# A small group's first matrix in matmuls of 512 columns, and one of its weight splits handed to a DMA

## The chip, the cores and the metric

The kernel runs on one core of a Trainium2 chip. The time is that of one execution on the device, in microseconds (us), and a kernel's time is the median of several executions. Columns of a matmul are the elements of the moving operand for each of the 128 partitions; the stationary operand is the weight that is loaded into the array ahead of it.

## The reference

```
x   = attention(q, packed keys)                       # [2304, 512]
x   = silu(x @ w_in) @ w_out                          # [2304, 512]
P   = sinkhorn(exp(x @ w_gate))                       # [2304, 8], eight rounds
out = 0
for e in range(8):
    h    = maximum(x @ w1[e], 0)                      # 512 -> 1024
    out += P[:, e:e+1] * (h @ w2[e])                  # 1024 -> 512
```

All of it is in float32. The kernel holds a float32 operand as a high part (`h`, in the matrix engine's type float32r) and a low part (`l`, what the high part leaves), and makes a product of three: high by high, high by low and low by high. An instruction of VectorE, `lo = raw - hi`, behind one of ScalarE, `hi = raw`, is called a split here (lines 144 and 145).

## The kernel before

The 2304 tokens of the last part are worked on in three groups: a small one of 256 tokens (two blocks of 128, called T0), and then two of 1024. The change is in the small group alone. It has 16 steps (`s` = 0 to 15, `G0` = 16): a step is one expert `e` and one half `fh` of its 1024 hidden columns, so each step has two weight matrices of 512 x 512, `w1` and `w2`, each loaded in two halves `j` of 256 rows (`load_w1`, `load_w2`, lines 773 to 787).

A step runs in four slots. Even slots run `up0(s, j)`, 24 matmuls of 256 columns (line 999): for two blocks `i` of 128 hidden rows and four blocks `k` of the 512 inputs, `wh` by `xs[0]` (the tokens' high part), `wh` by `xs[1]` (their low part) and `wl` by `xs[0]`. Behind them ScalarE makes the high part of the hidden values, `relu(ps)` (line 1002), and VectorE the low part, `max(ps, 0) - hi` (line 1003). Odd slots run `down0(s - 1, tt)` for one token block `tt`, 12 matmuls of 512 columns (line 1018), with the hidden values of the step before as stationary operand; the first six use what came of `up0(s - 1, 0)`, the last six what came of `up0(s - 1, 1)`. So TensorE is given up, down, up, down, and the hidden values of a step have some slots to be made in.

Each slot also takes one piece of other work. `w1_split(s + 1)` has its two halves in slots 0 and 1, `w2_split(s)` in slots 2 and 3 (of the last step, 15, in slots 0 and 1). In odd slots from step 1 on, `sinkhorn` takes one piece (about one round: a matmul `cs` with ones, line 1231, and eight small VectorE instructions). From step 9 on `x_forms` makes the sums of token blocks that the second group needs (lines 949 to 958, each followed by a split into `xf`); what is left of it is done at the end of step 14. The pieces of step 0 are made ahead, in `pre0`, beside the last matmuls of the stage before.

TensorE, VectorE and ScalarE run their instructions in exactly the order in which the code writes them (`manual_schedule`); the order of loads on the DMA queue of SyncE is the scheduler's. GpSimd has no work in this part. Buffers: 16 units of 128 x 1024 (`wp`) hold the split weights in turn, and `m` in PSUM holds two results of `up0` for each of the two `j`.

Of the kernel before, what the change touches and what calls it, by code (L numbers as in the profile page):

```python
# [14 lines left out]
ALU = mybir.AluOpType  # L15
# [89 lines left out]
def fused_kernel(  # L105
# [745 lines left out]
    def w1_split(s):  # L851
        w1t[s] = []
        for j in range(2):
            w1t[s].append(halves("w1", s, j, raw1[s, j]))
            if s + 1 < G0:
                load_w1(s + 1, j)
            yield
# [118 lines left out]
    xs, h0 = [], {}  # L976

    def pre0():

        t = [st["gh"].tile([128, 4, 256], F32R, tag="gh", name=f"xs{n}") for n in range(2)]  # L980
        xs.extend(t)
        for k in range(4):
            for n, (sb, c, _) in enumerate(T0):
                o = slice(128 * n, 128 * n + 128)
                split(t[0][:, k, o], t[1][:, k, o], x2[sb][k][:, c:c + 128])
            yield
        yield from w1_split(0)
        yield from w2_split(0)

    def up0(s, j):  # L990
        tag = "xz"[j]
        ps = st["m"].tile([128, 512], F32, tag=tag, name=f"u0{s}{j}").rearrange("p (i n) -> p i n", i=2)
        for i in range(2):
            n = 0
            f = slice(128 * (2 * j + i), 128 * (2 * j + i) + 128)
            for k in range(4):
                wh, wl = w1t[s][k // 2]
# [308 lines left out]
    with tc.manual_schedule(engines={mybir.EngineType.PE, mybir.EngineType.DVE, mybir.EngineType.Activation}):  # L1306
        for i, (c, b) in enumerate(seq):
# [14 lines left out]
            for half in range(2):  # L1322
# [3 lines left out]
                if c == NC - 1 and b == order[c][2] and half == 0:  # L1326
                    a2b_st.close()
                    open_("gh", 6)
# [66 lines left out]
    with tc.manual_schedule(engines={mybir.EngineType.PE, mybir.EngineType.DVE, mybir.EngineType.Activation}):  # L1395
# [12 lines left out]
        st["m"], s_ = pool("pm", 2, space=PSUM, side="left", reuse_waits="tile"); ctx.enter_context(s_)  # L1408
# [6 lines left out]
        for s in range(G0 + 1):  # L1415
            wb = w2_split(s) if 0 < s < G0 else iter(())
            wa = w1_split(s + 1) if s + 1 < G0 else wb
            for slot in range(4):
# [12 lines left out]
                next(wa if slot < 2 else wb, None)  # L1431
# [13 lines left out]
        for name in ("acc", "r2", "gh", "po"):  # L1445
            closers[name].close()
        for name, n in (("hb", 6), ("hi", 3), ("lo", 3), ("rb", 2)):
            open_(name, n, keep=True)
# [59 lines left out]
```

## Time and profile before

| | |
|---|---|
| median of 3 runs | 1784.09 us (1783.89 to 1784.69) |
| the profiled execution's own time | 1784.24 us |
| its span, from the first instruction to the last | 1782.5 us |
| TensorE busy | 1768.4 us, 99% of the span |
| VectorE busy | 1438.2 us, 81% |
| ScalarE busy | 1065.7 us, 60% |
| granted TensorE clock, as a share of full speed | 1.00 |

The times of the profiled execution and of the span differ by 1.7 us, which lie around the first and the last instruction. Matmuls overlap: one that is listed with 0.39 us may be followed by the next after 0.23 us, so the pace of TensorE is read from the starts of its matmuls and not from their durations.

### The profile page before, as it was taken

Reading aid. Unit: us, or ns where it says so; the run is one execution under the profiler, and the core shown is the slowest. Engines: PE = TensorE matmul, PEld = TensorE weight load, DVE = VectorE, ACT = ScalarE, POOL = GpSimd, SP = SyncE. Lnnn points to the kernel's source line nnn. Section 1 sums busy time; section 2 is a strip of 40 time slices with the busy share of each in tenths; the row PEclk is TensorE's granted clock in tenths of the full one; section 3 lists DMA queues with packets and bytes.
Section 4 is the critical chain, followed back from the end, with each engine's and each line's share of the span. In section 5 each row is a group of like instructions: output and inputs, shape, how many; then the busy total and the mean of one; then the engine's idle time right before and its main releaser. Section 6 shows DMA issues by size and latency. Waiting matters only on the chain.

```text
span 1782.5 us, 25390 instructions
## 1 busy us (share of the span) xinstructions
PE 1768.4 (99%) x9580; PEld 1509.7 (85%) x9580; DVE 1438.2 (81%) x1918; ACT 1065.7 (60%) x1694; POOL 1.0 (0%) x8
## 2 busy tenths in 40 slices
PE   8999999999999999999999999999999999999998
PEld 5899999989998888888888888888888888888887
DVE  7968796759676988899889999887777777777778
ACT  6766675644453666665666666656555555555555
POOL 0000000000000000000000000000000000000000
PEclk9999999999999999999999999999999999999999
DMA  9326676975664655465544455964454444545432
GB/s 363 129 95 214 247 262 249 331 255 172 221 210 161 229 180 183 160 203 186 199 162 171 172 186 196 322 222 167 155 174 165 154 154 147 170 155 172 148 130 95
DMA packets 141498, 341.75 MB, mean 192 GB/s; under 512 B 11952, under 2 KB 49472, under 8 KB 140480
## 3 DMA queue, kind: packets, MB, share of 16 engines
q1 hardware_dynamic: 141376, 340.14, 54.9%
q8 instruction: 75, 1.23, 0.3%
q14 instruction: 47, 0.39, 0.1%
HBM read 256.66 MB, written 83.44 MB: 191 GB/s over the span
## 4 chain that ended last, share of the span: by engine, by line
PE 95%; DVE 3%; ACT 1%; issue 1%; DMA 0%; DVEq 0%; SPq 0%; ACTq 0%
PE d L1106 34%; PE X L1154 20%; PE Z L1154 10%; PE g2w L689 8%; PE g L600 5%; PE Y L1154 5%; PE u L999 5%; PE d L1018 4%; PE g L654 3%; PE u L193 1%; PE s L193 0%; DMA kq<-in_kT_dram 0%; PE warm L203 0%; PE lg L1188 0%; DVE w2l L145 0%
## 5 line engine op out<-in xcount | busy, mean ns | idle before, releaser
L145 DVE TENSOR_TENSOR lo<-hb,hi 128x1024 fp32r<-128x1024 f32 x224 | 273.6, 1221 | 33.5 <-ACT hi L144 32.5
L1106 PE MATMUL d<-hi,w2f 128*128 128x512 f32 x896 | 294.2, 389 | 0.0
L1154 PE MATMUL X<-xf,w1l 128*128 128x512 f32 x1152 | 276.9, 389 | 0.0
L144 ACT CAST hi<-hb 128x1024 fp32r<-128x1024 f32 x224 | 235.3, 1052 | 64.8 <-PE d L1106 59.4
L1154 PEld LDWEIGHTS X<-xf,w1l 128*128 128x128 f32 x1152 | 216.2, 188 | 44.9
L1114 ACT COPY M<-d 128x512 f32<-128x512 f32 x234 | 137.3, 588 | 143.1 <-PE d L1106 139.8
L1118 DVE TENSOR_TENSOR M<-d,M 128x512 f32<-128x512 f32 x204 | 140.1, 687 | 100.6 <-PE d L1106 100.6
L1106 PEld LDWEIGHTS d<-hi,w2f 128*128 128x128 f32 x896 | 168.1, 188 | 34.9
L1106 PE MATMUL d<-lo,w2f 128*128 128x512 f32 x448 | 174.3, 389 | 0.0
L1106 PE MATMUL d<-hi,w2l 128*128 128x512 f32 x512 | 167.7, 389 | 0.0
L689 PE MATMUL g2w<-ring,woh 128*128 128x384 f32 x576 | 147.5, 337 | 0.0
L1102 ACT COPY d<-M 128x512 f32<-128x512 f32 x216 | 127.1, 590 | 20.9 <-DVE M L1118 19.5
L1106 PE MATMUL d<-hi,w2g 128*128 128x512 f32 x384 | 125.7, 389 | 0.0
L1106 PEld LDWEIGHTS d<-hi,w2l 128*128 128x128 f32 x512 | 96.2, 188 | 20.3 <-ACT d L1102 0.4
L689 PEld LDWEIGHTS g2w<-ring,woh 128*128 128x128 f32 x576 | 102.9, 188 | 8.6 <-issue 7.5
L1161 ACT COPY cp<-X 128x512 f32<-128x512 f32 x128 | 74.3, 581 | 46.5 <-PE X L1154 46.2
L1106 PE MATMUL d<-lo,w2l 128*128 128x512 f32 x256 | 99.6, 389 | 0.0
L1106 PEld LDWEIGHTS d<-lo,w2f 128*128 128x128 f32 x448 | 84.1, 188 | 17.5
L1154 PE MATMUL Y<-xf,w1f 128*128 128x512 f32 x384 | 97.3, 389 | 0.0
L689 PE MATMUL g2w<-ring,wol 128*128 128x384 f32 x288 | 96.3, 334 | 0.0
L999 PE MATMUL u<-xs,w1h 128*128 128x256 f32 x512 | 94.4, 285 | 0.0
L144 ACT CAST w1f<-rb 128x512 fp32r<-128x512 f32 x96 | 59.8, 624 | 54.9 <-PE d L1106 40.3
(220 smaller groups left out, 3482.0 us busy)
## 6 DMA issues: line engine op xcount, KB each, us to landing
r<-in_moe_w_dram SPq DMA_DIRECT2D x128, 512.0 KB, 3.9
w1l<-w1d SPq DMA_DIRECT2D x128, 512.0 KB, 4.2
w1d<-po SPq DMA_DIRECT2D x64, 512.0 KB, 4.4
w2d<-w2f SPq DMA_DIRECT2D x64, 512.0 KB, 4.1
w2l<-w2d SPq DMA_DIRECT2D x64, 512.0 KB, 3.6
rb<-in_moe_w_dram SPq DMA_DIRECT2D x96, 256.0 KB, 2.6
sb<-in_moe_w_dram SPq DMA_DIRECT2D x48, 256.0 KB, 2.7
pb<-pd SPq DMA_DIRECT2D x16, 512.0 KB, 5.2
```

The lines of the kernel that those rows point to most:

```text
L144: act.copy(out=hi, in_=raw)
L145: eng.tensor_tensor(out=lo, in0=raw, in1=hi.bitcast(F32), op=ALU.subtract)
L600: pe.matmul(ps, lhs[:, fs], rhs, start=(n == 0), stop=(n == 5))
L689: pe.matmul(ps[:, :TW], lhs[:, f % 2, ds], ring[f // 2][:, 2 * (f % 2) + rhs, q], start=(n == 0 and not on), stop=(n == 11), skip_group_ch ...
L999: pe.matmul(ps[:, i], w[:, k % 2, f], x[:, k], start=(n == 0), stop=(n == 11))
L1018: pe.matmul(ps, h[:, l, f % 2, 128 * tt:128 * tt + 128], w[:, f % 2], start=(fh == 0 and n == 0), stop=(fh == 1 and n == 11))
L1102: act.copy(out=ps, in_=m)
L1106: pe.matmul(ps, w[:, l, c, 128 * d:128 * d + 128], r[:, c], start=(n == 0 and not seed), stop=(n == 5), skip_group_check=seed)
L1114: act.copy(out=m, in_=ps)
L1118: dve.tensor_tensor(m, ps, m, op=ALU.add)
L1154: pe.matmul(ps, w[:, l, c, 128 * i:128 * i + 128], x[:, r, c], start=(n == 0 and p in (1, 7)), stop=(n == 5), skip_group_check=p in (2, 6, ...
L1161: act.copy(out=t, in_=ps)
```

## The change

`up0` multiplies each high weight by the tokens' high and low parts in one matmul of 512 columns: the two parts now lie side by side in one tile `xs`. The result has two halves of 256 columns; the low weight's matmul, still of 256 columns, is added into the first. A new `sum0` adds the two halves (a copy by ScalarE, an addition by VectorE) into a tile `us` in SBUF, and `relu0`, one slot later, makes the high and low hidden values from it (in the last step in the same slot). The result of an `up0` takes two banks of PSUM in place of one, and two are held in place of four, so four banks as before.

For the steps from 1 on, the low part of the first half of `w1` no longer comes from VectorE: ScalarE writes `l = -h`, and a DMA of GpSimd's queue adds the raw weight to it from HBM a second time. The splits move: the first half of `w1` for step `s + 2` is made in slot 3 of step `s`, its second half in slot 0 of the step behind, the halves of `w2` in slots 1 and 2 of their own step. For the last step that is a slot later for `w2` than before.

```
@@ pre0, w1_split: the split by DMA @@
+            if s == 0 or j == 1:
+                w1t[s].append(halves("w1", s, j, raw1[s, j]))
+            else:
+                h = unit([128, 2, 512], F32R, f"w1h{s}{j}")
+                l = unit([128, 2, 512], F32R, f"w1l{s}{j}")
+                act.copy(out=h, in_=raw1[s, j])
+                act.activation(l, h.bitcast(F32), AF.Copy, scale=-1.0)
+                _, e, fh = steps[s]
+                nc.gpsimd.dma_start(l, w1[e, 256 * j:256 * j + 256, FH * fh:FH * fh + FH]
+                                    .rearrange("(c p) f -> p c f", p=128), accum_op=ALU.add)
+                w1t[s].append((h, l))
...
-        yield from w1_split(0)
-        yield from w2_split(0)
+        for g, n in ((w1s, 0), (w1s, 0), (w2s, 0), (w2s, 0), (w1s, 1)):
+            next(g[n])
+            yield
...
     def up0(s, j):
-        tag = "xz"[j]
-        ps = st["m"].tile([128, 512], F32, tag=tag, name=f"u0{s}{j}").rearrange("p (i n) -> p i n", i=2)
+        ps = st["u0"].tile([128, 2, 512], F32, tag="u0", name=f"u0{s}{j}")
         for i in range(2):
-            n = 0
             f = slice(128 * (2 * j + i), 128 * (2 * j + i) + 128)
             for k in range(4):
-                wh, wl = w1t[s][k // 2]
-                for w, x in ((wh, xs[0]), (wh, xs[1]), (wl, xs[0])):
-                    pe.matmul(ps[:, i], w[:, k % 2, f], x[:, k], start=(n == 0), stop=(n == 11))
-                    n += 1
+                pe.matmul(ps[:, i], w1t[s][k // 2][0][:, k % 2, f], xs[0][:, k].rearrange("p l n -> p (l n)"),
+                          start=(k == 0), stop=(k == 3), skip_group_check=True)
+            for k in range(4):
+                pe.matmul(ps[:, i, 0:256], w1t[s][k // 2][1][:, k % 2, f], xs[0][:, k, 0],
+                          start=False, stop=(k == 3), skip_group_check=True)
+        h0[s, j] = ps
+
+    def sum0(s, j):
+        u0, ps = st["S"].tile([128, 2, 256], F32, tag="S", name=f"us{s}{j}"), h0[s, j]
+        act.copy(out=u0, in_=ps[:, :, 256:])
+        dve.tensor_tensor(u0, ps[:, :, 0:256], u0, op=ALU.add)
+        h0[s, j] = u0
+
+    def relu0(s, j):
+        if (s, j) in done0:
+            return
+        done0.add((s, j))
+        u0 = h0[s, j]
         t = st["gh"].tile([128, 2, 2, 256], F32R, tag="gh", name=f"h0{s}{j}")
-        act.activation(t[:, 0], ps, AF.Relu)
-        dve.scalar_tensor_tensor(t[:, 1], ps, 0.0, t[:, 0].bitcast(F32), op0=ALU.max, op1=ALU.subtract)
+        act.activation(t[:, 0], u0, AF.Relu)
+        dve.scalar_tensor_tensor(t[:, 1], u0, 0.0, t[:, 0].bitcast(F32), op0=ALU.max, op1=ALU.subtract)
...
         for s in range(G0 + 1):
-            wb = w2_split(s) if 0 < s < G0 else iter(())
-            wa = w1_split(s + 1) if s + 1 < G0 else wb
...
-                next(wa if slot < 2 else wb, None)
+                g, n = ((w1s, s + 1), (w2s, s), (w2s, s), (w1s, s + 2))[slot]
+                if n < G0:
+                    next(g[n], None)
+                if slot % 2 == 0:
+                    sum0(s, slot // 2)
+                if slot % 2 or s == G0 - 1:
+                    relu0(s, slot // 2)
```

The instructions move on three queues. ScalarE in step 12 (its work from the even slot 0 on; the first number in a name is the step, the last digit `j`), before:

```order
L1002 ACTIVATE h0120_5893<-u0120_5868 128x512
L144 CAST w1h130_5896<-r1_130_5782 128x1024
L144 CAST w1h131_5915<-r1_131_5801 128x1024
L144 CAST xf14_5922<-xr101_5579 128x512
L1002 ACTIVATE h0121_5950<-u0121_5925 128x512
L144 CAST w2h120_5953<-r2_120_5839 128x1024
L144 CAST w2h121_5976<-r2_121_5862 128x1024
L1002 ACTIVATE h0130_6007<-u0130_5982 128x512
```

and in the changed program:

```order
L1017 COPY us120_5792<-u0120_5769 128x512
L144 CAST w2h120_5808<-r2_120_5703 128x1024
L1027 ACTIVATE h0120_5814<-us120_5792 128x512
L144 CAST xf14_5818<-xr101_5502 128x512
L144 CAST w2h121_5838<-r2_121_5733 128x1024
L1017 COPY us121_5844<-u0121_5821 128x512
L859 CAST w1h140_5864<-r1_140_5760 128x1024
L860 ACTIVATE w1l140_5865<-w1h140_5864 128x1024
L1027 ACTIVATE h0121_5871<-us121_5844 128x512
L144 CAST w1h141_5891<-r1_141_5790 128x1024
L1017 COPY us130_5897<-u0130_5874 128x512
```

A copy `us` now stands first behind each `up0`, the high hidden value comes a slot later, and the weights of slot 3 are those of two steps ahead, with a second instruction for the low part.

VectorE where the small group ends: the last three sums of `x_forms` (`xr`), the values of step 15 (`h0150`, `h0151`) and its splits of `w2`, before:

```order
L952 TENSOR_TENSOR xr110_5959<-xr111_5960,xr110_5959 128x512
L145 TENSOR_TENSOR xf17_5842<-xr110_5959,xf17_5842 128x512
L955 TENSOR_TENSOR xr111_5960<-xr111_5960,xr110_5959 128x512
L145 TENSOR_TENSOR xf16_5865<-xr111_5960,xf16_5865 128x512
L958 TENSOR_TENSOR xr111_5960<-xr111_5960 128x512
L145 TENSOR_TENSOR xf14_5922<-xr111_5960,xf14_5922 128x512
L1003 SCALAR_TENSOR_TENSOR h0150_6239<-u0150_6214,h0150_6239 128x512
L145 TENSOR_TENSOR w2l150_6243<-r2_150_6177,w2h150_6242 128x1024
L145 TENSOR_TENSOR w2l151_6260<-r2_151_6199,w2h151_6259 128x1024
L1003 SCALAR_TENSOR_TENSOR h0151_6288<-u0151_6263,h0151_6288 128x512
```

and in the changed program:

```order
L962 TENSOR_TENSOR xr110_5847<-xr111_5848,xr110_5847 128x512
L145 TENSOR_TENSOR xf17_5739<-xr110_5847,xf17_5739 128x512
L965 TENSOR_TENSOR xr111_5848<-xr111_5848,xr110_5847 128x512
L145 TENSOR_TENSOR xf16_5766<-xr111_5848,xf16_5766 128x512
L968 TENSOR_TENSOR xr111_5848<-xr111_5848 128x512
L145 TENSOR_TENSOR xf14_5818<-xr111_5848,xf14_5818 128x512
L1018 TENSOR_TENSOR us150_6098<-u0150_6081,us150_6098 128x512
L1028 SCALAR_TENSOR_TENSOR h0150_6101<-us150_6098,h0150_6101 128x512
L145 TENSOR_TENSOR w2l150_6118<-r2_150_6016,w2h150_6117 128x1024
L145 TENSOR_TENSOR w2l151_6139<-r2_151_6044,w2h151_6138 128x1024
L1018 TENSOR_TENSOR us151_6142<-u0151_6121,us151_6142 128x512
L1028 SCALAR_TENSOR_TENSOR h0151_6145<-us151_6142,h0151_6145 128x512
```

Two additions `us` stand ahead of the hidden values, the second behind both splits. Just ahead of the first row shown stands, before, the second split of `w2` of step 14 behind an accumulation `acc01`; in the changed program the low value `h0141` behind that accumulation.

GpSimd, whose queue held nothing of this part, has the 15 adding DMAs of steps 1 to 15; the last five of them are:

```order
L862 DMA w1l110_5545<-in_moe2_w1_dram 128x2x512
L862 DMA w1l120_5648<-in_moe2_w1_dram 128x2x512
L862 DMA w1l130_5756<-in_moe2_w1_dram 128x2x512
L862 DMA w1l140_5865<-in_moe2_w1_dram 128x2x512
L862 DMA w1l150_5964<-in_moe2_w1_dram 128x2x512
```

No instruction stands between them: each waits for its own low part and then goes out.

## Rows read from the trace of the kernel before

**Rows 1.** Page, parts 1 and 4: busy engines, and the chain that ended last.

```profile
PE 1768.4 (99%) x9580; PEld 1509.7 (85%) x9580; DVE 1438.2 (81%) x1918; ACT 1065.7 (60%) x1694; POOL 1.0 (0%) x8
...
PE 95%; DVE 3%; ACT 1%; issue 1%; DMA 0%; DVEq 0%; SPq 0%; ACTq 0%
```

**Rows 2.** Windows, small group: us, busy per engine, clock, DMA share, GB/s.

```profile
374.10:558.60 184.50, 183.99 (x1181) 166.69 (x1179) 137.45 (x203) 89.81 (x116) 0.00 (x0) 1.00 0.63 208
```

**Rows 3.** Groups by shape in that stretch: busy us, mean ns, idle before.

```profile
L999 PE MATMUL u<-xs,w1h 128*128 128x256 f32 x512 | 94.4, 285 | 0.0
...
L145 DVE TENSOR_TENSOR w1l<-r,w1h 128x1024 fp32r<-128x1024 f32 x30 | 36.2, 1220 | 5.1 <-ACT w1h L144 4.8
...
L144 ACT CAST w1h<-r 128x1024 fp32r<-128x1024 f32 x30 | 30.2, 1046 | 1.8 <-DMA r<-in_moe_w_dram 1.8
...
L1003 DVE SCALAR_TENSOR_TENSOR h<-u,h 128x512 fp32r<-128x512 f32 x32 | 22.0, 688 | 25.3 <-ACT h L1002 25.3
L1002 ACT ACTIVATE h<-u 128x512 fp32r<-128x512 f32 x32 | 19.1, 598 | 69.9 <-PE u L999 69.9
```

**Rows 4.** Timeline of TensorE, an up and a down slot: start us, us.

```profile
490.57 0.40 PE L999 MATMUL u<-xs,w1h 128*128 128x256 f32 x2
...
493.44 0.40 PE L1018 MATMUL d<-w2h,h 128*128 128x512 f32 x1
...
496.19 0.40 PE L999 MATMUL u<-xs,w1h 128*128 128x256 f32 x2
```

**Rows 5.** Timeline of TensorE, right behind the small group.

```profile
558.63 2.88 PE L1154 MATMUL X<-xf,w1f 128*128 128x512 f32 x12
561.35 2.88 PE L1154 MATMUL Y<-xf,w1f 128*128 128x512 f32 x12
```

**Rows 6.** Timeline of TensorE, the first three up slots.

```profile
374.14 0.50 PE L999 MATMUL u<-xs,w1h 128*128 128x256 f32 x2
...
381.29 0.38 PE L999 MATMUL u<-xs,w1l 128*128 128x256 f32 x1 [0.16 <-DVE w1l L145]
...
383.30 0.40 PE L1018 MATMUL d<-w2h,h 128*128 128x512 f32 x1
```

**Rows 7.** Timeline of SyncE's queue, ahead of the small group.

```profile
366.34 0.38 SPq L776 DMA_DIRECT2D r<-in_moe_w_dram  x1
```

**Rows 8.** DMA issues from 368 to 374 us: count, KB, median us to landing.

```profile
r<-in_moe_w_dram SPq DMA_DIRECT2D x3, 512.0 KB, 5.3
...
rb<-in_moe_w_dram SPq DMA_DIRECT2D x1, 256.0 KB, 7.5
```

**Rows 9.** DMA issues in the small group.

```profile
r<-in_moe_w_dram SPq DMA_DIRECT2D x58, 512.0 KB, 3.9
```

**Rows 10.** Timeline of VectorE, one sinkhorn round and what follows.

```profile
422.05 0.17 DVE L1233 TENSOR_SCALAR rc<-cs 128x8 f32<-128x8 f32 x1
...
424.57 1.22 DVE L145 TENSOR_TENSOR w1l<-r,w1h 128x1024 fp32r<-128x1024 f32 x1
```

**Rows 11.** Timeline of ScalarE at the small group's end.

```profile
549.76 0.62 ACT L144 CAST xf<-xr 128x512 fp32r<-128x512 f32 x1 [1.36 <-DVE xr L958]
550.29 0.59 ACT L1002 ACTIVATE h<-u 128x512 fp32r<-128x512 f32 x1
```

**Rows 12.** Timeline of VectorE at the small group's end.

```profile
550.41 0.69 DVE L145 TENSOR_TENSOR xf<-xr,xf 128x512 fp32r<-128x512 f32 x1 [0.69 <-ACT xf L144]
...
551.85 2.36 DVE L145 TENSOR_TENSOR w2l<-r,w2h 128x1024 fp32r<-128x1024 f32 x2
554.13 0.68 DVE L1003 SCALAR_TENSOR_TENSOR h<-u,h 128x512 fp32r<-128x512 f32 x1
```

**Rows 13.** Timeline of TensorE there, in down0 of step 15.

```profile
552.16 0.61 PE L1018 MATMUL d<-w2h,h 128*128 128x512 f32 x2
553.13 0.50 PE L1018 MATMUL d<-w2l,h 128*128 128x512 f32 x1 [0.35 <-DVE w2l L145]
...
554.87 0.73 PE L1018 MATMUL d<-w2h,h 128*128 128x512 f32 x2
```

More of the change, by code (lines that the diff above doesn't have):

```diff
@@ L853, in w1_split @@
         for j in range(2):
-            w1t[s].append(halves("w1", s, j, raw1[s, j]))
+            if s == 0 or j == 1:
[9 more added lines that the diff above has]
+                w1t[s].append((h, l))
             if s + 1 < G0:
@@ L974, in x_store @@
         nc.sync.dma_start(xfd[p][:, :, c], t.bitcast(F32))
-    xs, h0 = [], {}
+    xs, h0, done0 = [], {}, set()
+    w1s = {s: w1_split(s) for s in range(G0)}
+    w2s = {s: w2_split(s) for s in range(G0)}
     def pre0():
-        t = [st["gh"].tile([128, 4, 256], F32R, tag="gh", name=f"xs{n}") for n in range(2)]
-        xs.extend(t)
+        xs.append(st["xx"].tile([128, 4, 2, 256], F32R, tag="xx", name="xs"))
         for k in range(4):
@@ L984, in pre0 @@
                 o = slice(128 * n, 128 * n + 128)
-                split(t[0][:, k, o], t[1][:, k, o], x2[sb][k][:, c:c + 128])
+                split(xs[0][:, k, 0, o], xs[0][:, k, 1, o], x2[sb][k][:, c:c + 128])
             yield
-        yield from w1_split(0)
-        yield from w2_split(0)
+        for g, n in ((w1s, 0), (w1s, 0), (w2s, 0), (w2s, 0), (w1s, 1)):
+            next(g[n])
+            yield
     def up0(s, j):
-        tag = "xz"[j]
-        ps = st["m"].tile([128, 512], F32, tag=tag, name=f"u0{s}{j}").rearrange("p (i n) -> p i n", i=2)
+        ps = st["u0"].tile([128, 2, 512], F32, tag="u0", name=f"u0{s}{j}")
         for i in range(2):
-            n = 0
             f = slice(128 * (2 * j + i), 128 * (2 * j + i) + 128)
             for k in range(4):
-                wh, wl = w1t[s][k // 2]
-                for w, x in ((wh, xs[0]), (wh, xs[1]), (wl, xs[0])):
-                    pe.matmul(ps[:, i], w[:, k % 2, f], x[:, k], start=(n == 0), stop=(n == 11))
-                    n += 1
+                pe.matmul(ps[:, i], w1t[s][k // 2][0][:, k % 2, f], xs[0][:, k].rearrange("p l n -> p (l n)"),
[14 more added lines that the diff above has]
+        u0 = h0[s, j]
         t = st["gh"].tile([128, 2, 2, 256], F32R, tag="gh", name=f"h0{s}{j}")
-        act.activation(t[:, 0], ps, AF.Relu)
-        dve.scalar_tensor_tensor(t[:, 1], ps, 0.0, t[:, 0].bitcast(F32), op0=ALU.max, op1=ALU.subtract)
+        act.activation(t[:, 0], u0, AF.Relu)
+        dve.scalar_tensor_tensor(t[:, 1], u0, 0.0, t[:, 0].bitcast(F32), op0=ALU.max, op1=ALU.subtract)
         h0[s, j] = t
@@ L1327, in fused_kernel @@
                     a2b_st.close()
-                    open_("gh", 6)
+                    open_("xx", 1)
+                    open_("gh", 4)
                     open_("r2", 2)
@@ L1407, in fused_kernel @@
         open_("acc", 2 * LATE)
-        st["m"], s_ = pool("pm", 2, space=PSUM, side="left", reuse_waits="tile"); ctx.enter_context(s_)
+        st["u0"], u0_st = pool("pu", 2, space=PSUM, side="left", reuse_waits="tile")
         def chain(*gens):
@@ L1444, in fused_kernel @@
                     w1_get(G0, p)
-        for name in ("acc", "r2", "gh", "po"):
+        for name in ("acc", "r2", "gh", "xx", "po"):
             closers[name].close()
+        u0_st.close()
+        st["m"], s_ = pool("pm", 2, space=PSUM, side="left", reuse_waits="tile"); ctx.enter_context(s_)
         for name, n in (("hb", 6), ("hi", 3), ("lo", 3), ("rb", 2)):
```

## The prediction

> **What bounds the kernel now.** I read the page first: TensorE is busy 99% of the span, and 95% of the chain that ended last is its work [rows 1]. Then the windows for the stretch that the change touches, the small group from 374.1 to 558.6 us: the clock is granted in full (1.00, the upper of its two levels, 2.4 GHz), TensorE is busy 183.99 of 184.50 us, VectorE 137.45, ScalarE 89.81 and the DMA engines 0.63 of the time [rows 2]. So TensorE alone sets the time here. The timeline of TensorE shows how: an up slot takes 493.44 - 490.57 = 2.87 us, a down slot 496.19 - 493.44 = 2.75 us, one straight behind the other [rows 4]. Idle time stands only at the two ends: the first three up slots take 383.30 - 374.14 = 9.16 us, 0.55 over three times 2.87, with a wait for a low weight from VectorE [rows 6], and in the down slots of step 15 TensorE waits for splits and hidden values that VectorE makes late: the 25 matmuls from 552.16 to 558.63 [rows 5, 13] take 6.47 us where 25 at a down slot's pace (0.2292, below) take 5.73, so 0.74 us, most of it ahead of 553.13 and the rest around 554.87. A gain can therefore come from a shorter up slot (32 of them) and from these ends; nothing that VectorE, ScalarE or a DMA saves counts by itself.
>
> **The pace of TensorE.** 24 matmuls of 256 columns in 2.87 us are 0.1196 us each [rows 4]. Twelve of 512 columns take 561.35 - 558.63 = 2.72 us behind the small group, 0.2267 each [rows 5], and 2.75 in a down slot, 0.2292 each [rows 4]. Two of 256 thus cost 0.2392, and one of 512 in their place saves 0.0100 to 0.0125 us. An up slot after the change has 8 of 512 and 8 of 256 columns: 8 x 0.2292 + 8 x 0.1196 = 2.79 us, or 2.77 by the other pace. The saving is 0.08 or 0.10 us a slot and 2.6 or 3.2 us over 32 slots. I take 2.6: in the new slot the wide matmuls stand in runs of four behind narrow ones, as they stand behind narrow ones in the down slot, where they are at the slower pace. Below, the bound is no saving at all, if switching between widths costs what it saves.
>
> The Trainium skill (TensorE: Matmul & The Clock Gate, Back-to-back issue gap) gives a warm matmul N/2.4 + 2.5 ns, so the fixed part that one matmul fewer saves is 2.5 ns. By that the 256 pairs would save 0.6 us in place of 2.6, and the sum at the end would be 1784.6 us; the rows above, with 10 to 12.5 ns a pair, do not agree with it, and they decide.
>
> **The other engines over the whole stretch.** VectorE loses 15 splits of 1.220 us and gains 32 additions; the nearest row for one, an instruction with a PSUM and an SBUF operand of the same size, is the low hidden value at 0.688 [rows 3]: -18.3 + 22.0 = +3.7 us. ScalarE gains 32 copies at the price of a relu from PSUM, 0.598, and 15 instructions `l = -h` at that of a weight's cast, 1.046 [rows 3]: +34.8 us. That makes about 141 and 125 of 182 us, both under TensorE, so it costs nothing while each piece has slots to spare. The cover is TensorE's own slots: what comes of an up slot is wanted one down and one up slot later, 5.5 us on; the chain for it grows by a copy and an addition, 0.598 + 0.688 = 1.3 us, to 2.6 us. That fits, except at three places.
>
> **The adding DMA in the steady state.** ScalarE makes `l = -h` in slot 3 of step s behind the copy for `sum0`: about 0.8 + 2 x 1.046 = 2.9 us into the slot, or one down slot later (5.6 us) in the early steps in which ScalarE first copies a finished sum. The low weight is first used in step s + 2, behind four wide matmuls (0.92 us): 2.75 + 2 x (2.79 + 2.75) + 0.92 = 14.75 us after the slot began. The DMA has 14.75 - 2.9 = 11.9 us, at worst 9.1. A plain load of the same 512 KB lands in 3.9 us in this stretch, the median of 58 [rows 9], and the slowest row near it is 7.5 [rows 8]. The trace has no adding DMA and none of GpSimd's queue; the bounds are 3.9 and, if reading the destination too doubles it, 7.8 (15 at twice the slowest row). I take it as hidden.
>
> **The start, -0.3.** The first adding DMA is tighter. The raw half for step 1 is issued at 366.34 [rows 7] and lands 5.3 us later at that time's median [rows 8], 371.6; ScalarE's two instructions end at 373.7. The first use is at 374.14 + 2 x 2.79 + 0.92 = 380.6, 6.9 us later, while loads there take 5.3 to 7.5 us [rows 8]. If it lands in time the present 0.55 us of wait goes; at 9 us it is 2 us of wait in its place. I put it at the near side, 0.25 left of the 0.55. Bounds: -0.55 and +1.5.
>
> **The sinkhorn rounds, +0.4.** From one round's first instruction to the next split VectorE takes 424.57 - 422.05 = 2.52 us [rows 10]. In these steps it now has two rounds, three splits, two additions and two low hidden values in order: 2 x 2.52 + 3 x 1.220 + 4 x 0.688 = 11.45 us, in a step of 11.1 us plus two short matmuls of the rounds. So VectorE runs full for the few steps that rounds take. What is queued behind a round is the low value of the second up slot: it comes 2.52 + 0.69 = 3.2 us after the round starts and is wanted by the ninth matmul of the next step's first down slot, 2.79 + 8 x 0.2292 = 4.6 us after the slot's end. Some 1 us is spare, and a round that starts later than that makes TensorE wait. Bounds: 0, and 1.2 for one split's length; I take 0.4, an estimate nearer the lower end since 1 us is spare.
>
> **The end, +0.9.** Here the order decides. Count from the start of step 14's second up slot. The slot takes 2.79, its last matmul ends 0.285 - 0.12 = 0.17 later [rows 3, 4], and copy, addition and the first difference of `x_forms` (priced as an addition) bring it to 5.0; that form's cast and split, 6.3. The accumulation, released by the down slot at 5.54, follows to 7.0, the low hidden value to 7.6, and the three forms left take about 1.97 each (a wait of 1.36 and a cast of 0.62 [rows 11]): VectorE is through at 13.5. TensorE comes to the first down slot of step 15 at 3 x (2.79 + 2.75) = 16.6. Between stand, in order, copy (done 13.3) and addition (14.2) of step 15's first half, relu (14.8), low value (15.5), the casts of `w2` (15.8, 16.7; ScalarE), its low parts (17.0, 18.2), and the second addition, which stands behind both of them (18.8), relu (19.45), low value (20.15). TensorE's second matmul wants the first low part and starts at 17.05 in place of 16.85; its seventh would start at 18.2 and wants the relu at 19.45; its ninth wants the low value at 20.2 instead of 19.95. Together 1.7 us of wait against 0.7 now. Now, the relu follows the last form's cast directly [rows 11] and the splits follow the low value [rows 12], two steps fewer in the chain. Bounds: all of it gone (-0.7), and twice the new wait (+2.7).
>
> **The sum.** -2.6 - 0.3 + 0.4 + 0.9 = -1.6 us. From the profiled execution's 1784.24 us (0.15 over the median) that is 1782.6 us. With every term at its better end it is -3.2 - 0.55 - 0.7 = -4.45, 1779.8; with start, rounds and end at their worse ends -2.6 + 1.5 + 1.2 + 2.7 = +2.8, 1787.0.
>
> **The rivals.** *All waits go* (faster): the wide matmuls run at 0.2267, the first DMA lands in time, and the forms end some 2 us sooner than I count, so that the second addition does not come late: 1779.8 us. For it: VectorE and ScalarE wait for each other at the end for much of the time [rows 11, 12], which leaves room. Against it: the second addition stands behind both splits whatever the forms do.
>
> *No saving in width*: 1784.24 - 0.3 + 0.4 + 0.9 = 1785.2 us. The rows speak against it, with 0.01 us a pair in two places [rows 4, 5].
>
> *The late ends eat the gain*: start, rounds and end at their worse ends, 1787.0 us. It decides where the first DMA takes over 9 us and the end's chain is 2 us longer than counted.
>
> *The adding DMA is late in every step* (slower): the low weight then holds TensorE once in each of 15 steps, since it works in order and nothing else can go ahead. It decides from 11.9 us between `l = -h` and landing (9.1 in the early steps), about three times the 3.9 of a plain load; at 14 us it is 2.1 x 15 = 31 us, less the 1.6 of the sum, so about 1814 us. For it: nothing here shows what reading, adding and writing back costs, and the DMA engines are already busy 0.63 of the time [rows 2]. Against it: 9 to 12 us of room, and only one such transfer in a step. The Trainium skill (SBUF — State Buffer, SBUF: two separate sides) warns that a DMA from GpSimd's queue stalls while VectorE runs an instruction that takes both its ports, for it can't write its descriptors. No run here shows whether VectorE's instructions in this stretch do that.
>
> **How the numbers follow.** A difference under 0.2%, 3.6 us, is about what a measurement can't tell from no change. I give my forecast 0.60, no saving in width 0.06 and the late ends 0.07, all three within 0.2% of before (1780.5 to 1787.7); all waits gone 0.15, just faster; the DMA late in each step 0.12, slower. So faster 0.15, same 0.73, slower 0.12. The time is that of the likeliest, 1782.6 us. The range reaches from 1779.8 to 1787.0, where the two cases at the ends lie, and leaves out the late DMA and what little lies under 1779.8.
>
> **What would show it.** In the changed profile an up slot of 2.77 to 2.79 us behind an unchanged down slot of 2.75 shows the width term, and the start of the first matmul behind the group (558.63 now [rows 5]) the whole sum: 557.0. A wait of TensorE for a DMA at the third up slot shows the start, gaps behind a down slot's eighth matmul in the sinkhorn steps the rounds, and waits for VectorE at the second, seventh and ninth matmul of the first down slot of step 15 the end. My prediction is wrong if TensorE waits for a DMA in step after step, if the narrow matmuls slow down beside the wide ones, or if the large groups' part, which I leave unchanged, moves by more than a microsecond.

## The result, and the profile after

The changed kernel takes 1795.19 us (median of four, 1794.24 to 1795.82) beside 1784.21 us for the kernel before (median of four): a ratio of 1.0061 with a 95% interval of 1.0043 to 1.0078. It is slower by 11 us, 0.6%, and outside the range that was forecast (1782.6, in 1779.8 to 1787.0). The profiled execution took 1795.29 us, its span 1793.5.

The page, parts 1 and 4 (the last row is the chain that ended last):

```profile
PE 1769.3 (99%) x9324; PEld 1497.5 (83%) x9324; DVE 1439.6 (80%) x1935; ACT 1100.0 (61%) x1741; POOL 19.4 (1%) x23
...
PE 91%; DMA 4%; DVE 2%; issue 2%; ACT 1%; SPq 0%; DVEq 0%; POOLq 0%; ACTq 0%
```

Beside [rows 1], TensorE is as busy as before, but its share of the chain has gone from 95% to 91%, and DMA has 4% where it had none. Where, the timeline of TensorE shows. First a steady up slot and down slot (start us, us; the matmul of line 1008 is the wide one, that of 1011 the narrow one):

```profile
487.08 1.07 PE L1008 MATMUL u<-xs,w1h 128*128 128x512 f32 x4
...
489.86 0.40 PE L1043 MATMUL d<-w2h,h 128*128 128x512 f32 x1
...
492.62 0.62 PE L1008 MATMUL u<-xs,w1h 128*128 128x512 f32 x2
```

The up slot is 489.86 - 487.08 = 2.78 us, the down slot 2.76: the width saves 0.08 to 0.09 us a slot where [rows 4] had 2.87. The first three up slots look otherwise:

```profile
374.54 0.97 PE L1008 MATMUL u<-xs,w1h 128*128 128x512 f32 x3
...
380.24 1.09 PE L1008 MATMUL u<-xs,w1h 128*128 128x512 f32 x4
385.48 1.23 PE L1011 MATMUL u<-xs,w1l 128*128 128x256 f32 x4 [4.14 <-DMA w1l<-in_moe_w_dram]
386.50 1.91 PE L1008 MATMUL u<-xs,w1h 128*128 128x512 f32 x4
388.21 1.05 PE L1011 MATMUL u<-xs,w1l 128*128 128x256 f32 x4
389.06 0.63 PE L1043 MATMUL d<-w2h,h 128*128 128x512 f32 x1
...
392.91 0.66 PE L1228 MATMUL lt<-ident,lgs 128*128 128x128 f32 x5
```

TensorE stands still for 4.14 us, waiting for the low weight of step 1. Then four wide matmuls take 388.21 - 386.50 = 1.71 us, 0.43 each where the steady slot has 0.23, and the down slot behind takes 392.91 - 389.06 = 3.85 us. The windows (us, busy time of PE, PEld, DVE, ACT and POOL, then granted clock, DMA share, GB/s) show at which clock:

```profile
380.00:385.40 5.40, 1.34 (x8) 0.81 (x6) 1.73 (x3) 3.10 (x4) 0.00 (x0) 0.92 0.98 269
385.40:387.00 1.60, 1.52 (x6) 1.43 (x7) 0.00 (x0) 0.33 (x1) 1.23 (x1) 0.50 0.56 132
...
391.00:393.00 2.00, 2.00 (x9) 1.55 (x9) 0.00 (x0) 1.29 (x2) 0.00 (x0) 0.90 1.07 251
393.00:396.00 3.00, 3.00 (x21) 2.66 (x20) 2.53 (x6) 0.00 (x0) 0.00 (x0) 1.00 0.91 253
```

Behind the wait the granted clock is 0.50, the lower level of 1.2 GHz, and it is back at 1.00 from about 391.4 us (0.90 over the two us from 391). The 0.92 over the stretch with the wait shows that it fell while TensorE still stood. The Trainium skill (TensorE: Matmul & The Clock Gate, HAM oscillation — how this bites in real kernels) describes this: a wait for a DMA between groups of matmuls costs more than itself, since the next group starts cold. This trace agrees here, with 0.50 behind a wait of 4.14 us.

The two DMA queues from 370 to 575 us (packets, MB, share of 16 engines; q1 is SyncE's, q0 GpSimd's with the adding DMAs), the issues in the same stretch (KB each, median us from issue to landing), and that of the first adding DMA alone:

```profile
q1 hardware_dynamic: 20294, 41.46, 60.8%
q0 software_dynamic: 4080, 7.87, 22.2%
...
r<-in_moe_w_dram SPq DMA_DIRECT2D x60, 512.0 KB, 5.9
w1l<-in_moe_w_dram POOLq DMA_DIRECT2D x15, 512.0 KB, 8.7
...
w1l<-in_moe_w_dram POOLq DMA_DIRECT2D x1, 512.0 KB, 12.0
```

An adding DMA lands in 8.7 us where a raw load took 3.9 [rows 9], and the raw loads beside it now take 5.9. Two more of the fifteen, in steps 8 and 14, come too late for TensorE:

```profile
468.40 1.07 PE L1008 MATMUL u<-xs,w1h 128*128 128x512 f32 x4
471.27 0.74 PE L1011 MATMUL u<-xs,w1l 128*128 128x256 f32 x4 [1.80 <-DMA w1l<-in_moe_w_dram]
...
539.72 0.74 PE L1011 MATMUL u<-xs,w1l 128*128 128x256 f32 x4 [0.88 <-DMA w1l<-in_moe_w_dram]
```

Their DMAs went out at 460.33 and 530.29, some 9.0 and 8.4 us ahead of the first use, and landed after 10.9 and 9.4 us. Behind the wait of 1.80 us the clock did not fall (a window, columns as above):

```profile
460.00:480.00 20.00, 18.20 (x93) 15.16 (x92) 12.84 (x16) 12.60 (x17) 2.44 (x2) 1.00 0.92 264
```

And the last 36 down matmuls of the group, 558.33 to 569.07, with ScalarE ahead of them (second fence):

```profile
558.33 0.40 PE L1043 MATMUL d<-w2h,h 128*128 128x512 f32 x1
...
562.18 0.50 PE L1043 MATMUL d<-w2l,h 128*128 128x512 f32 x1 [0.68 <-DVE w2l L145]
...
564.57 0.50 PE L1043 MATMUL d<-w2h,h 128*128 128x512 f32 x1 [0.97 <-ACT h L1027]
...
569.07 1.29 PE L1179 MATMUL X<-xf,w1f 128*128 128x512 f32 x5
```

```profile
557.31 0.62 ACT L144 CAST xf<-xr 128x512 fp32r<-128x512 f32 x1 [1.36 <-DVE xr L968]
557.84 0.58 ACT L1017 COPY us<-u 128x512 f32<-128x512 f32 x1
```

They take 10.74 us, 2.49 over three down slots of 2.75, where before it was 0.74 over. ScalarE's copy for step 15's first half stands behind the last cast of `x_forms` and starts at 557.84, though TensorE was done with that half's up slot at 552.78.

Set against the pace of each slot, the small group's 194.53 us (184.49 before) come out as follows; the last 0.2 us lie in the other slots, and 1.0 us more before and behind the group.

| where | over the pace before | after | difference |
|---|---|---|---|
| 32 up slots, 2.87 to 2.79 us (2.78 in most) | | | -2.6 |
| first three up slots, wait and lower clock | 0.55 | 6.15 | +5.6 |
| the down slot behind them, lower clock | 0 | 1.10 | +1.1 |
| steps 8 and 14, low weight late | 0 | 2.05 and 1.14 | +3.2 |
| one down slot at 528.67, hidden value late | 0 | 0.79 | +0.8 |
| last 36 down matmuls | 0.74 | 2.49 | +1.75 |

The late hidden value at 528.67 stands on ScalarE behind the adding DMA's own preparation. A form's cast waited 2.36 us there for VectorE and ended at 526.4; a cast of `w2`, the copy of the sum, the cast of `w1` and `l = -h` (1.06 us) followed, and the relu ran from 529.78 to 530.39, where TensorE wanted it at 530.05.

### The profile page after: what moved, and what is told of

It is laid out like the page before. It is cut to its first block, busy times and chain, and to the rows that moved or that the text cites. A ratio compares the mean times of both kernels' runs of the same rounds, so it can differ in the third digit from the quotient of the medians.

```text
span 1793.5 us, 24924 instructions
## 1 busy us (share of the span) xinstructions
PE 1769.3 (99%) x9324; PEld 1497.5 (83%) x9324; DVE 1439.6 (80%) x1935; ACT 1100.0 (61%) x1741; POOL 19.4 (1%) x23
## 4 chain that ended last, share of the span: by engine, by line
PE 91%; DMA 4%; DVE 2%; issue 2%; ACT 1%; SPq 0%; DVEq 0%; POOLq 0%; ACTq 0%
PE d L1131 33%; PE X L1179 19%; PE Z L1179 10%; PE g2w L689 7%; PE g L600 5%; PE Y L1179 5%; PE d L1043 4%; PE g L654 3%; PE u L1008 2%; DMA w1l<-in_moe_w_dram 2%; PE u L1011 1%; PE u L193 1%; DMA rawout<-in_moe_w_out_dram 1%; DMA v<-in_v_dram 1%; DMA q<-in_qT_dram 0%
## 5 line engine op out<-in xcount | busy, mean ns | idle before, releaser
L1179 PE MATMUL X<-xf,w1f 128*128 128x512 f32 x384 | 92.2, 389 | 0.0
```

Of the source, the lines that this page charges most:

```text
L1179: pe.matmul(ps, w[:, l, c, 128 * i:128 * i + 128], x[:, r, c], start=(n == 0 and p in (1, 7)), stop=(n == 5), skip_group_check=p in (2, 6, ...
```

## The experiments

The theory was that the adding DMA is the loss: it lands late, the longest wait lowers the clock, and its load on the DMA engines delays the raw weights. The rivals were a fixed cost of GpSimd's queue, any added transfer whether it adds or not, and, without the DMA, the moved splits and the sums on VectorE and ScalarE.

Each median is followed by its ratio to the kernel before, run beside it, with the 95% interval. A slot is "over" by what it takes beyond its pace: 2.79 us for an up slot, 2.75 for a down slot, or 2.90 for a down slot with the two short matmuls of a sinkhorn round. A form is one sum of `x_forms` with its split; an accumulation adds what came of a down slot into `acc`.

**Step 1 by VectorE.**

```
-            if s == 0 or j == 1:
+            if s <= 1 or j == 1:
```

> One DMA of the fifteen is taken away: step 1's first weight is split as before, its low part by VectorE; from step 2 on the adding DMA stays. Theory (the first adding DMA is late and the wait lowers the clock): the third up slot falls from 8.82 us to about 3 and the down slot behind it from 3.85 to 2.75, the granted clock stays at 1.00 from 381 us on, and the time falls by 6.5 to 7.5 us to about 1788. Rival, a fixed cost of the first transfer on GpSimd's queue: the wait and the fall of the clock only move one step on, to the up slots of step 2, and the time stays at 1793 to 1795. Rival, the moved splits or the sums load ScalarE and VectorE too much: the time does not change, 1795.

1788.43 us, 1.0023 (1.0013 to 1.0033): 6.8 less than the changed kernel, as the theory had it. The third up slot is 2.81 us and the clock there 1.00. But something of what the rival expected shows too: the up slot of step 2 is now 0.9 us over. At step 8 the wait is 1.94 us in place of 1.80, and this time the clock fell behind it, so that this up slot and the down slot behind it are 3.8 us over (TensorE, and a window, columns as above):

```profile
464.63 0.74 PE L1011 MATMUL u<-xs,w1l 128*128 128x256 f32 x4 [1.94 <-DMA w1l<-in_moe_w_dram]
...
466.00:468.00 2.00, 2.00 (x8) 1.71 (x8) 0.90 (x1) 1.35 (x2) 0.13 (x1) 0.50 1.08 338
```

So the lateness is not the first transfer's as such. In the changed kernel other transfers go out within a microsecond of the two that came latest for TensorE: two stores of 512 KB (`x2d`) beside the first, and two loads of 512 KB (`pb`, 8.9 us to landing) beside that of step 8. The busy share of the DMA engines alone does not tell the places apart: in the 6 us behind the issue it was 0.97 for the first, which took 12.0 us, and 1.04 for that of step 3, which took 6.0. No run took these other transfers away, so that they make the DMA late is argued and not shown.

**No adding DMA.**

```
-            if s == 0 or j == 1:
+            if True:
```

> All adding DMAs are taken away: every split is done on ScalarE and VectorE as before, while the wide matmuls, the sums and the slots of the changed kernel stay. Theory (the adding DMA is the loss): no wait for a transfer in the group, up slots 2.78 us, raw loads of the group back at about 4 us; the width gives 2.9 us, the end costs 1.0 to 1.75 us: 1782 to 1784. Rival, the sums beside all splits fill VectorE (before 137.45 us busy of 184.50, with 16 times two sums more and 64 splits): waits for VectorE in the up slots, up to 1800. Rival, the moved splits cost and not the DMA: above 1788.

1787.37 us, 1.0016 (1.0007 to 1.0025). The DMA with what it moved is worth 7.8 of the 11 us. No up slot waits any more and raw loads land in 4.2 us, but the time misses the 1782 to 1784 of the theory and is not under that of before: five down slots wait for the low hidden value, 1.26, three times 0.44, and 1.17 us, and the end is 2.48 us over as in the changed kernel. The first of them, on TensorE and then on VectorE:

```profile
409.31 0.72 PE L1043 MATMUL d<-w2h,h 128*128 128x512 f32 x2 [0.98 <-DVE h L1028]
```

```profile
404.29 0.68 DVE L1018 TENSOR_TENSOR us<-u,us 128x512 f32<-128x512 f32 x1
404.89 0.16 DVE L1258 TENSOR_SCALAR rc<-cs 128x8 f32<-128x8 f32 x1
...
407.44 1.21 DVE L145 TENSOR_TENSOR w1l<-r,w1h 128x1024 fp32r<-128x1024 f32 x1
408.57 0.68 DVE L1028 SCALAR_TENSOR_TENSOR h<-us,h 128x512 fp32r<-128x512 f32 x1
```

The sum is done at 405.0, but a sinkhorn round and a split stand between it and the low value `h`, which TensorE needed at 408.2. The first rival had VectorE too full, but put the waits in the up slots. So the DMA that made the low weights late also kept VectorE free enough for the sums.

**A plain DMA in its place.**

```
-                                    .rearrange("(c p) f -> p c f", p=128), accum_op=ALU.add)
+                                    .rearrange("(c p) f -> p c f", p=128))
```

> The DMA on GpSimd's queue no longer adds: it writes the raw weight over the tile, so that the low part is not the difference but the whole weight; commands, bytes, place and waits are otherwise those of the changed kernel. Theory (adding costs about twice the engine time of a plain transfer and so lands late): the landing falls from a median of 8.7 us to 4 to 6, the first one from 12 to about 6 to 7.5, the group's queue time from 2.5% of the span to about 1.3%, and most of the loss at step 1 goes: 1785 to 1788. Rival, any transfer more at that place and on that queue is late, added or not: landing 8 us or more, clock falls at 385 us again, 1793 to 1796.

1790.35 us, 1.0034 (1.0021 to 1.0046), between the two expectations. Its queue over the small group (packets, MB, share of 16 engines, 370 to 575 us), the median landing, and the first transfer alone:

```profile
q0 software_dynamic: 4080, 7.87, 12.9%
...
w1l<-in_moe_w_dram POOLq DMA_DIRECT2D x15, 512.0 KB, 6.5
...
w1l<-in_moe_w_dram POOLq DMA_DIRECT2D x1, 512.0 KB, 11.0
```

The same stretch of the changed kernel has 22.2% for the same bytes, so adding costs 1.7 times the engine time (SyncE's queue in that kernel, 41.46 MB at 60.8%, has 1.47% per MB, the adding DMAs 2.8). Most of the lateness at steps 8 and 14 comes of that: here step 8 is 0.65 us over and step 14 not at all. But the first transfer still lands in 11.0 us without adding, where it took 12.0 with it; the wait and the lower clock at step 1 stay, and cost 4.2 us in the up slots and 0.9 in the down slot. There a plain transfer on this queue is late too. The queue alone does not make a transfer slow: the second plain copy landed in 4.0 us, beside 3.9 for raw loads before [rows 9]. What a plain load on SyncE's queue would have taken in the first one's place, no run shows.

**Half the bytes.**

```
-                nc.gpsimd.dma_start(l, w1[e, 256 * j:256 * j + 256, FH * fh:FH * fh + FH]
-                                    .rearrange("(c p) f -> p c f", p=128), accum_op=ALU.add)
+                nc.gpsimd.dma_start(l[:, 0], w1[e, 256 * j:256 * j + 128, FH * fh:FH * fh + FH], accum_op=ALU.add)
```

> The adding DMA moves only the first 128 of its 256 rows (256 KB); the other half of the low weight is left at minus the high part. Theory (cost by the byte on full DMA engines): the landing falls to 5 to 7 us in the median and the first to 7 to 8.5, steps 8 and 14 wait no more, the time is 1785 to 1789. Rival, a fixed cost of each transfer on that queue or of the stall of its issue: the landing stays at 8 to 9 us and the time at 1793 to 1796.

1788.68 us, 1.0021 (1.0012 to 1.003), with a median landing of 6.6 us and no wait at steps 8 and 14, as the theory had it. But half the bytes took only 2.1 of the 8.7 us off the landing, so most of it does not go with the bytes of this transfer; the 4.0 us of the plain copy above speak against a fixed cost of the queue, which leaves the time beside other transfers, not tested apart. The first still takes 9.8 us, more than expected; TensorE waits 1.86 us for it, the clock falls to 0.50, and the first three up slots are 3.7 us over.

**TensorE kept busy through the wait.**

```
-            for k in range(4):
+            for k in [0] * (18 * (s == 1 and j == 0 and i == 0)) + list(range(4)):
                 pe.matmul(ps[:, i], w1t[s][k // 2][0][:, k % 2, f], xs[0][:, k].rearrange("p l n -> p (l n)"),
```

> The changed kernel with its fifteen adding DMAs; in the third up slot the first wide matmul is done 19 times instead of once (each begins the sum anew, so the result is the same). These 18 take about 4.1 us, as long as PE stood still there for the low weight. Theory (the wait costs its 4.1 us and then about 3 us more, since the granted clock falls to 0.50 behind it): PE idles under 0.5 us there, the clock stays at 1.00 from 385 to 391 us, the third up slot is 6.8 to 7.2 us and the down slot behind it 2.75, and the time falls by 2.5 to 3.3 us to about 1792.3. Rival, the slow matmuls come from something else there (the transfers, ScalarE, the low weight's arrival): nothing changes or the 18 matmuls come on top, 1795 to 1799.

1791.18 us, 1.0039 (1.0023 to 1.0054): 18 matmuls more, and 4.0 us less than the changed kernel. Its timeline of TensorE and one of its windows:

```profile
379.80 5.17 PE L1008 MATMUL u<-xs,w1h 128*128 128x512 f32 x22
...
385.55 1.09 PE L1008 MATMUL u<-xs,w1h 128*128 128x512 f32 x4
386.48 0.64 PE L1011 MATMUL u<-xs,w1l 128*128 128x256 f32 x4
386.95 0.40 PE L1043 MATMUL d<-w2h,h 128*128 128x512 f32 x1
```

```profile
385.40:387.00 1.60, 1.60 (x12) 1.42 (x11) 0.00 (x0) 0.88 (x1) 1.02 (x1) 1.00 0.66 131
```

The low weight is as late as it was (12.0 us), the wide matmuls take 0.23 us behind it and the down slot 2.76: the clock alone cost the third up slot and the down slot 8.82 + 3.85 - 7.15 - 2.76 = 2.8 us. The other 1.2 us are less time lost at steps 8 and 14 (0.3 each), a down slot at 525 us (0.2) and an earlier start of the group (0.45).

The next four leave out the adding DMA, as the second one did (`if True` in the line shown there), to see what the sums cost by themselves.

**The width alone, splits in the old slots.**

```
-                g, n = ((w1s, s + 1), (w2s, s), (w2s, s), (w1s, s + 2))[slot]
+                g, n = ((w1s, s + 1), (w1s, s + 1), (w2s, s), (w2s, s))[slot]
+                if s == G0 - 1:
+                    g, n = w2s, s
```

> One part alone: the 512-column matmuls with their sums, every split on ScalarE and VectorE, and the splits in the slots of the kernel before (first weight in the first two slots, second in the last two). Without the adding DMA the changed kernel took 1787.4 us, 2.8 more than before, with down slots 1.25, 3 times 0.43 and 1.15 us late for the values' low part and an end 1.75 us longer. Theory (the sums put the values later on VectorE, and the values' low part stands behind a split and a sinkhorn round): the same waits are there whatever the slots of the splits, 1786 to 1788.5. Rival, the moved splits are what is late: without the move the waits go and the time is 1781.5 to 1783.5.

The first half of `w1` for step 1 is then no longer made ahead in `pre0` either. 1789.04 us, 1.0027 (1.0018 to 1.0037), slower still. The five waits are as long (1.26, 0.43, 0.42, 0.43, 1.17 us), though in the first the eighth matmul now waits for a low part of `w2`; so to take the move back does not take them away. The end is 5.54 us over instead of 2.48: two waits of 1.33 and 1.54 us for hidden values, and behind them nine matmuls in 3.65 us (0.50 is the clock from 560 to 562), some 1.6 us more than at their pace.

**The forms sooner.**

```
-                if s >= 9 and slot:
+                if s >= 8 and slot:
```

> No adding DMA; the token forms of the next group begin one step sooner (from the ninth step on instead of the tenth), so that about one is left for the end of the fifteenth step instead of four; all else as in the kernel without adding DMA (1787.4). Theory (the end is late because the sum and values of the last step stand behind four forms on VectorE and ScalarE): the last 36 matmuls fall from 10.73 us to 8.3 to 9.0 and the time by 1.5 to 2.3 us to about 1785.5. Rival, the end is set by the last splits of the second weight, or the forms only crowd the steps before: 1787 or more.

1785.81 us, 1.0009 (1.0001 to 1.0018), as expected. No wait is left at the end. But new ones of 1.13, 0.53 and 1.09 us came where forms and accumulations meet, at 499, 511 and 545 us, for one at 521.

**The values ahead of the split.**

```
+                if slot % 2:
+                    relu0(s, slot // 2)
                 if n < G0:
                     next(g[n], None)
                 if slot % 2 == 0:
                     sum0(s, slot // 2)
-                if slot % 2 or s == G0 - 1:
+                if s == G0 - 1:
                     relu0(s, slot // 2)
```

> No adding DMA; in the second and fourth slot of each step the values (their high part on ScalarE, low part on VectorE) are put ahead of the slot's weight split instead of behind it. Theory (the down slots wait since the low part of the values stands behind a split of 1.22 us on VectorE): the waits of 1.25, 3 times 0.43 and 1.15 us go, the end stays at about 10.7, and the time falls by 3 to 3.8 us to about 1784. Rival, VectorE as a whole is too full in the sinkhorn steps, so that the split is then late in place of the values: 1786.5 to 1788.

1787.40 us, 1.0019 (1.001 to 1.0028): no gain. The wait at 406 us went, but the three in the sinkhorn steps stayed at 0.42 to 0.49, the one at 521 grew to 1.71 and the end to 3.48 us. The theory named the split alone; the round ahead of it is enough: of the one at 418 us the sum was done at 417.0, a round followed, and the low value ran from 419.42 to 420.10, where the ninth matmul wanted it at 419.8.

**Both.** The two edits above together.

> No adding DMA; values ahead of the split and token forms one step sooner, both. Theory (the width is worth 2.9 us, and the waits behind it come from the order on VectorE and ScalarE alone): no wait of PE over 0.3 us is left in the group, 1781.5 to 1782.8, 0.1 to 0.2% under before. Rival, VectorE is full once the forms and the splits meet in the sinkhorn steps: 1784 or more.

1788.40 us, 1.0024 (1.0015 to 1.0033), where the theory had 1781.5 to 1782.8. A down slot at 510 us is 2.42 us over and one at 545 us 3.98. The latter on TensorE, with a window behind it (columns as above), and ScalarE at the time:

```profile
548.98 0.50 PE L1043 MATMUL d<-w2h,h 128*128 128x512 f32 x1 [1.99 <-ACT h L1027]
...
552.00:554.00 2.00, 2.00 (x6) 1.52 (x6) 1.76 (x3) 1.52 (x2) 0.00 (x0) 0.50 1.01 389
```

```profile
547.77 0.62 ACT L144 CAST xf<-xr 128x512 fp32r<-128x512 f32 x1 [2.01 <-DVE xr L968]
548.30 0.62 ACT L1027 ACTIVATE h<-us 128x512 fp32r<-128x512 f32 x1
```

The relu stands behind a form's cast, and that waits 2.0 us for VectorE. Here ScalarE and VectorE wait for each other in order. Of the three reorderings none took the waits away without new ones elsewhere. Behind this one the clock fell as well, and the up slot behind it took 3.66 us; of the loss in the two slots some 1.7 us are the clock.

**The DMA only where it is in time.** Eleven steps keep it (the expectation counts ten).

```
-            if s == 0 or j == 1:
+            if s in (0, 1, 2, 8, 14) or j == 1:
```

> The adding DMA stays in ten of the fifteen steps; in steps 1, 2, 8 and 14, where it came late in the changed kernel or in the one with step 1 split by VectorE (and in step 0 as there), VectorE makes the low weight. Theory (only the late landings cost, and where the DMA is in time it relieves VectorE in the sinkhorn steps): no wait for a transfer, no wait in the sinkhorn steps except where the split returned, about 0.8 us in one down slot and 1.75 us more at the end than before: 1783.8 to 1785.2. Rival, the waits move to other steps, as from step 1 to step 2 when one DMA was taken away: 1786 to 1789.

1784.57 us, 1.0002 (0.9993 to 1.0011): no different from before. No low weight is late and no sinkhorn step waits; one down slot at 519 us is 1.27 us over and the end 2.47.

**That, with the forms sooner.** The edit of `s >= 8` added.

> As the last, with the token forms of the next group one step sooner. Without adding DMAs that took the wait at the end away (2.48 us) and brought three waits of 0.5 to 1.1 us in the steps with forms and additions. Theory (VectorE, relieved by the DMA in most of these steps, has room for the forms): the end wait goes and the waits that come sum to under 1 us: 1781.8 to 1783.5. Rival, the forms are late or make late as much as they did without the DMA: 1784 or more.

1785.19 us, 1.0005 (0.9996 to 1.0014). Not the gain that the theory had: the end wait went, and four others of 0.7 to 1.6 us came, one of them for an adding DMA that landed in 9.4 us. Here the forms sooner move the waits and gain nothing.

**The last forms behind the values.** On the kernel with the DMA in eleven steps:

```
-            if s == G0 - 2:
-                for _ in xg:
-                    pass
...
                 for p in ORD[:AHEAD]:
                     w1_get(G0, p)
+                for _ in xg:
+                    pass
```

> As the kernel with the adding DMA in ten steps (1784.6), with one thing moved: the token forms that were finished at the end of the fifteenth step are left to the slots of the last step, so that two of the four stand behind the sums and values of that step instead of ahead of them. Theory (the end's longer wait is those two forms on ScalarE and VectorE ahead of the last step's sum): the last 36 matmuls fall from 10.72 us to 8.3 to 9.0, nothing else moves, and the time falls by 1.7 to 2.4 us to 1782.2 to 1783 (0.1% under before). Rival, the forms are then late for the next group's first products: the group ends sooner, but what follows it is longer by as much, 1784 to 1785.

1783.63 us beside 1784.69 for before: 0.9994 (0.9985 to 1.0003). The group's end on TensorE:

```profile
552.58 0.50 PE L1043 MATMUL d<-w2h,h 128*128 128x512 f32 x1 [0.34 <-ACT h L1027]
...
557.07 2.88 PE L1179 MATMUL X<-xf,w1f 128*128 128x512 f32 x12
```

The last 36 matmuls fall to 9.11 us, 0.86 over (8.3 to 9.0 us was expected), and what follows the group is no longer than in the kernel that it starts from. So the forms ahead of the last sum were most of the end's longer wait. The time misses the 1782.2 to 1783 of the theory. It is the lowest of these versions, with a median 1 us under before; the interval holds 1, so it is not shown to beat it.

## Why the prediction was wrong

**What failed** is the price of the adding DMA. The step was "I take it as hidden", with bounds of 3.9 and 7.8 us (15 at twice the slowest row), and for the first one "I put it at the near side", with +1.5 as the worse end. Both priced it from plain loads. Measured, it lands in 8.7 us (median) and 12.0 for the first, and costs 1.7 times a plain one's engine time. The room was about as counted: 7.7 us for the first, where 6.9 was counted, and 8.4 at the least in the other steps, where 9.1 was. Step 1 is the larger miss. The term was -0.3, and its up slots and the down slot behind them are 7.25 us over where 0.55 was before, +6.7. Of the 7.25, 4.1 is the wait and 2.8 the lower clock behind it, which the sum did not have at all. Steps 8 and 14 add 3.2, where the sum had nothing. The kernel before showed that the place was full. Its windows there (columns as above):

```profile
368.00:374.00 6.00, 6.00 (x67) 3.56 (x65) 3.15 (x4) 2.15 (x3) 0.00 (x0) 1.00 0.97 326
374.00:380.00 6.00, 6.00 (x52) 5.86 (x50) 2.38 (x3) 2.48 (x3) 0.00 (x0) 1.00 0.98 329
```

The 16 DMA engines were busy 0.97 and 0.98 of the time. I read their share over the whole group, 0.63 [rows 2], and took durations of transfers without asking what else the engines carry where the new one starts. The slowest row that I took, 7.5 us [rows 8], was one of 256 KB, half of what the adding DMA moves. Between the rows of that group stood the two stores that go out beside it, here before and after:

```profile
x2d<-x2a SPq DMA_DIRECT2D x2, 512.0 KB, 6.9
...
x2d<-x2a SPq DMA_DIRECT2D x2, 512.0 KB, 10.1
```

Half the bytes still took 9.8 us there, a plain copy 11.0.

**The width** (-2.6) was right: 2.78 us a slot, in the forecast 2.77 to 2.79. The Trainium skill (TensorE: Matmul & The Clock Gate, Back-to-back issue gap) gives N/2.4 + 2.5 ns for an isolated warm matmul; an estimate by that 2.5 ns would have left 2.85 us a slot, and this trace does not agree.

**The sinkhorn rounds** (+0.4): no wait in the changed kernel, the lower bound of the term. The count had the three splits a step that the DMA leaves. With the fourth back on VectorE (no adding DMA) the rounds cost 1.3 us, and 1.26 more at 406 us.

**Not in the sum** was the down slot at 528.67, +0.8: the prediction had ScalarE's two added instructions as covered there, and the hidden value came late behind them and a form.

**The end** (+0.9): the mechanism was right, the size was not. The second, seventh and ninth matmul of step 15 waited, as forecast, and the term measured 1.75 us. Of 2.49 us over the pace 1.7 were forecast. The count began with an addition that follows its copy at once; VectorE was still at a split of step 14:

```profile
547.66 1.22 DVE L145 TENSOR_TENSOR w2l<-r,w2h 128x1024 fp32r<-128x1024 f32 x1
548.79 0.68 DVE L1018 TENSOR_TENSOR us<-u,us 128x512 f32<-128x512 f32 x1
```

The copy ended at 547.43 + 0.59 = 548.02 and the addition began 0.8 us later. The count had VectorE through with the forms at 13.5; in the trace the last form's split begins at 557.96 and ends 14.2 us after the 544.45 from which the count runs, and what follows came some 0.6 us late, to the last low value (20.2 in the count, 20.8 in the trace).

**The rivals.** "The adding DMA is late in every step" named the cause and its sign with 0.12, at 1814 us; it was late in three of fifteen. "The late ends eat the gain" had two conditions: the first, a first DMA over 9 us, came true, but with 1.5 us for it; the other, an end's chain 2 us longer than counted, did not, for it was 0.6. The 15 instructions that issue the DMAs on GpSimd took nearly the same time throughout (ns, minimum, median, maximum):

```profile
L862 POOL DMA_DIRECT2D w1l<-in_moe_w_dram x15: 1213/1222/1332, 373.4 to 540.0; - x15
```

The Trainium skill (SBUF — State Buffer, SBUF: two separate sides) warned of a stall on that queue beside VectorE; these rows, 1213 to 1332 ns, show none.

The width's gain is real, but the sum puts a copy and an addition, on ScalarE and VectorE, behind each up slot. Where these engines also have rounds, accumulations and forms, the waits that come of it give the gain back: with the late DMAs taken away the kernel is at 1784.6 beside 1784.3 for before, with 1.27 us lost at 519 and 2.47 at the end.

## What to carry to other kernels

Price a transfer that is new to the kernel at the place where it starts: look at what else goes out there, how full the DMA engines are and the slowest landing of its own size, and take an adding one as nearly two plain ones (1.7 here). A wait of TensorE can cost more than itself, since the matmuls behind it may start at the lower clock (2.8 us behind 4.1 here); a bound for a late operand has to hold that too. Where a shorter matmul sequence puts another copy and addition between two engines that work in order, count what stands ahead of each hand-over in the fullest steps and not the mean load.

## What the runs showed of the hardware

Added into SBUF from HBM, 512 KB took 1.7 times the DMA engines' time of the same bytes copied (22.2% and 12.9% of 16 engines in one stretch), and landed in 6.0 to 12.0 us in the changed kernel. Behind a wait of 4.14 us the clock was granted at 0.50 for some 6 us (385.4 to about 391.4), and with TensorE kept busy through that wait it stayed at 1.00. Behind a wait of 1.80 us it stayed at 1.00 (step 8 of the changed kernel), and behind one of 1.94 us at the same step in the first experiment it fell. Of two waits of 1.86 us it fell behind one (half the bytes, at 381 us) and not behind the other ("Both", at 511 us). So the length of the wait alone does not decide; what does is left open.
